# A fused attention and expert kernel: scores and their copies ranked ahead, three small steps moved to other engines

## The chip, the core and the metric

One core of one Trainium2 chip runs the whole program. Its engines work side by side, each on a queue of its own that it takes strictly in order: TensorE (PE: matrix products and transposes; PEld is its weight load), VectorE (DVE), ScalarE (ACT), GpSimd (POOL), and SyncE (SP), which here only issues transfers. The metric is the device time of one execution in microseconds (us).

## What is computed

```python
def reference(**kwargs):
    attn_out = _attn_ref(**attn_kwargs)          # 4 batches, 8 heads, 576 x 64
    x = np.ascontiguousarray(attn_out.transpose(0, 2, 1, 3)).reshape(B * S, H * D)
    x = _moe_ref(x=x, **moe_kwargs)              # (x @ w_a) * (x @ w_b) @ w_out, 512 -> 1536 -> 512
    return _moe2_ref(x=x, **moe2_kwargs)         # each token to one of 8 experts, 512 -> 1024 -> 512

def _attn_ref(q, k, v):
    top_k = 32
    scores = scale * np.matmul(q, k.transpose(0, 1, 3, 2))
    kth = np.partition(scores, -top_k, axis=-1)[..., -top_k:-top_k + 1]
    scores = np.where(scores >= kth, scores, -1000000000.0)
    scores = scores - np.max(scores, axis=-1, keepdims=True)
    attn = np.exp(scores)
    attn = attn / (np.sum(attn, axis=-1, keepdims=True) + 1e-09)
    return np.matmul(attn, v).astype(np.float32)
```

So every row of 576 scores keeps its 32 largest, and the first dense layer (w_a, w_b, w_out) follows, then the experts.

## The kernel before

**Tiles and loops.** A batch has four head pairs. A unit is one head pair of a batch, or, in batch 0, one head pair and one of two groups of rows (group 0 with 320 of the 576 rows, group 1 with 256). That gives 8 units in batch 0, of which the first four are group 0, and 4 units in each later batch. A unit's group has four tiles of 128 query rows (two for each head, taken in pairs) and group 0 a fifth one (kind "M"); there are 144 tiles, 36 per batch, in 32 groups.

**One pair of tiles** (`attn_tiles`, `attn_out`). TensorE makes scores of one half of the keys into the tile `sp` (one buffer in PSUM), ScalarE copies them to `s` (L527), TensorE makes the other half into the same `sp`, ScalarE copies that too. VectorE forms the larger and the smaller of the two halves (`m` and `n`, L534 and L535), finds the 32 largest by rounds of MAX8 and MATCH_REPLACE8 (L546 to L573), and makes the masked numerators `am` with their sums (L601). For the exponential (`e`, ScalarE, L554) GpSimd makes the negative scaled maximum `nm` (L549). TensorE transposes `am` (L609 to L636), ScalarE copies the transposes to `aT` (L616 to L638), and at a group's end TensorE multiplies them with v (`pv`, L648 and L652).

**Normalization** (`attn_norm`). GpSimd adds 1e-9 to the sums (L671), VectorE takes reciprocals (L673), ScalarE spreads them (L674, L682), TensorE turns them to rows in `pv` (L690, L692). In batches 0 and 1 ScalarE then copies these to `rs` (L697) and GpSimd multiplies `xf` out of `xc` and `rs` (L698); in batches 2 and 3 VectorE multiplies straight from PSUM (L701).

**The dense layer** (`moe1`). It starts for a batch (in batch 0 for a group) when `xf` is there: ScalarE and GpSimd split `xf` into a high part `xh` (L716) and a remainder `xl` (L718); TensorE multiplies with w_a and w_b (L748) and with w_out (L778), three products for each, as the weights are split too. Before that the weights, which arrive as 64-bit words, go through 36 conversions (`conv`, L371 to L424): a load, two ScalarE and two VectorE steps (L385, L388), a product on GpSimd (L391), the split (L396, L397) and stores to the scratch tensors `ws` and `wos`, from which `moe1` loads its weights into `wt` (three buffers). The conversions borrow the buffers gT, gH, xh and xl of `moe1`. After each batch or group `gating` sorts the rows into `xsort`; at the end the experts follow (L1109, L1158).

**What sets the order.** All of this is recorded as operations with an engine, an assumed cost and a rank `pos` (10 per tile). A planner (`Plan.emit`) walks through them by its assumed times: an engine that is free takes, of the operations that are ready, the one with the lowest rank. The instructions are then written out in the order of the planned starts. The dense layer's products have rank 100000 and more, so they fill what attention leaves free on TensorE; its evacuations have rank -1. On the chip each engine keeps that order, whether or not the first in its queue is ready.

Of the kernel before, what the change touches and what calls it, by code (L numbers as in the profile page):

```python
# [14 lines left out]
AF = mybir.ActivationFunctionType  # L15
OP = mybir.AluOpType
# [4 lines left out]
SCALE = 0.125  # L21
# [163 lines left out]
def c_act(n, sbuf=False):  # L185
    return (95 if sbuf else 55) + n * 0.83
# [23 lines left out]
def fused_kernel(ctx: ExitStack, tc: tile.TileContext, q, k, v, w_a, w_b, w_out, w_gate, w1, w2, qx, kx, vx, out,  # L210
                 opts=None, dbg=None):
    nc = tc.nc
    opts = opts or {}
# [15 lines left out]
    HB = FB // 2  # L229
    CW = 512  # L230
    HALVES = opts.get("halves", (0,))
    FU = opts.get("fu", range(8))
    PE, ACT, DVE, POOL, SP = "PE", "ACT", "DVE", "POOL", "SP"

# [17 lines left out]
    P = P_.op  # L252
# [115 lines left out]
    def conv(src, pos):  # L368
        (zr, raw), (zf, f) = conv_bufs()
        fk = ("f", nconv[0])  # L370
        o = P(SP, c_dma(128 * CW * 8), pos, lambda: nc.sync.dma_start(raw().bitcast(I64), src), w=[(zr, "r")])  # L371
        if nconv[0] > opts.get("c0", 2):
            o.deps.add(U[0].mark)

        def words(i):
            return raw().bitcast(I32).rearrange("p (n t) -> p n t", t=2)[:, :, i]

        def hi():
            return words(1).bitcast(F32)

        def fi():
            return f().bitcast(I32)
        P(ACT, c_act(CW, True), pos, lambda: nc.scalar.activation(f(), hi(), AF.Abs, scale=2.0 ** -111),
          r=[(zr, "r")], w=[(zf, fk)])
        P(DVE, c_ts(CW), pos, lambda: nc.vector.tensor_scalar(  # L385
            fi(), fi(), 3, 0x7fffffff, op0=OP.logical_shift_left, op1=OP.bitwise_and), w=[(zf, fk)])
        P(ACT, c_act(CW, True), pos, lambda: nc.scalar.activation(hi(), hi(), AF.Sign), w=[(zr, "r")])
        P(DVE, c_dve(CW), pos, lambda: nc.vector.scalar_tensor_tensor(  # L388
            fi(), words(0), 29, fi(), op0=OP.logical_shift_right, op1=OP.bitwise_or),
          r=[(zr, "r")], w=[(zf, fk)], label=f"cv{nconv[0]}")  # L390
        P(POOL, c_pool(CW), pos, lambda: nc.gpsimd.tensor_mul(f(), f(), hi()), r=[(zr, "r")], w=[(zf, fk)])  # L391
        return (zf, fk), f, zr, raw
# [93 lines left out]
    def attn_tiles(lst, r, pos):  # L486
# [8 lines left out]
        if kind == "M":  # L495
            sp = T(p_ps, [128, 2, 512], F32, "sp", 1)

            def score():
# [4 lines left out]
                                               kp()[:, 64 + hf * HS:64 + (hf + 1) * HS], start=(x == 0),  # L503
                                               stop=(x == len(pr) - 1))
                return res
            P(PE, 980 if u.f else 900, pos, score, r=u.q + u.k, w=[sp],
              label=f"score{u.b}")
            P(ACT, c_act(S), pos, lambda: nc.scalar.copy(
                s()[:, 0, :].rearrange("p (a b) -> p a b", a=2), sp()[:, :, 0:HS]), r=[sp], w=[(s, (0, 0)), (s, (0, 1))],
              label="s")  # L510
        else:
            for hf in range(2):
                sp = T(p_ps, [128, 2, 512], F32, "sp", 1)

                def score(hf=hf, sp=sp):
# [6 lines left out]
                                                   kp()[a, k0 + hf * HS:k0 + (hf + 1) * HS], start=(x == 0),  # L522
                                                   stop=(x == len(pr) - 1))
                    return res
                P(PE, 780 if u.f else 540, pos, score, r=u.q + u.k, w=[sp],
                  label=f"score{u.b}")
                P(ACT, c_act(S), pos, lambda hf=hf, sp=sp: nc.scalar.copy(  # L527
                    s()[:, :, hf * HS:(hf + 1) * HS], sp()[:, :, 0:HS]), r=[sp], w=[(s, (h, hf)) for h in range(2)],
                  label="s")

# [14 lines left out]
        for h, (i, j, kind, _, c) in enumerate(lst):  # L545
            P(DVE, c_dve(HS), pos, lambda h=h, j=j: nc.vector.max(out=kt(j, 0, 8), in_=m()[:, h]), r=[(m, h)],  # L546
              w=[KT(j, 0)])
        nm = T(p_sml, [128, 2, 1], F32, "nm", 3)
        P(POOL, 180, pos - 5, lambda: nc.gpsimd.tensor_scalar(  # L549
            nm()[:, 0:nh], r.kt()[:, j0:j0 + nh, 0:1], -SCALE, None, op0=OP.mult),  # L550
          r=[KT(j0 + h, 0) for h in range(nh)], w=[nm])
        for h, (i, j, kind, _, c) in enumerate(lst):
            e = T(p_at, [128, S], F32, "e", opts.get("e", 3))
# [106 lines left out]
        return any(a <= i < b and i % m < n for a, b, n, m in opts.get("mk", ()))  # L660

    def b_norm(b):
        return b in opts.get("pn", (0, 1))

    def attn_norm(i, r, xf, pos):
        u, g, nt = r.u, r.g, r.nt
# [1 line left out]
        P(POOL, 170, pos, lambda: nc.gpsimd.tensor_sub(  # L668
            chk_t[:, i - nt + 1:i + 1], r.kt()[:, 0:nt, 47], r.kt()[:, 0:nt, 39]),
          r=[r.kt], w=[(CHK, i)])  # L670
        P(POOL, 180, pos - 20, lambda: nc.gpsimd.tensor_scalar(r.sum()[:, 0:nt], r.sum()[:, 0:nt], 1e-9, None, op0=OP.add),  # L671
          w=[r.sum])
        P(DVE, 100, pos - 20, lambda: nc.vector.reciprocal(r.sum()[:, 0:nt], r.sum()[:, 0:nt]), w=[r.sum])  # L673
        P(ACT, c_act(256, True), pos - 20, lambda: nc.scalar.copy(  # L674
# [863 lines left out]
```

## Time and profile before

| | us |
|---|---|
| median of 3 runs (1207.56 to 1209.87) | 1208.23 |
| the profiled execution | 1207.8 |
| its span, first to last instruction | 1206.1 |
| TensorE busy | 1082.9 (90%) |
| VectorE busy | 894.5 (74%) |
| ScalarE busy | 678.6 (56%) |
| GpSimd busy | 462.5 (38%) |

The sum in the prediction is made against the profiled execution: 1207.8 us, of which 1.7 lie outside its span, and 0.4 below the median. Shares over the whole span mix stages with different limits: attention runs from 5 to 796 us, the dense layer from 142 to some 900, the experts after it. Times in rows count from the start of the span. "Granted clock" is the share of TensorE's full speed that was granted; its two levels are 1.2 and 2.4 GHz (0.5 and 1.0), so a mean of 0.85 tells that it stood at the lower level for 30% of the stretch.

### The profile page before, as it was taken

The page shows a single profiled execution, that of the slowest core. Times are in us where ns is not written, and L with a number is a line of the kernel's source. Part 1 is how long each engine was busy: PE and PEld are TensorE (multiplying, and loading weights), DVE is VectorE, ACT ScalarE, POOL GpSimd, SP SyncE. Part 2 cuts the span into 40 slices and gives each one's busy share as a digit, 9 for nine tenths or more (in the row PEclk, how much of TensorE's full clock was granted, in tenths as well). Part 3 has the DMA queues.
Part 4 walks back from the last instruction along what each step waited for, and adds up shares of the span by engine and source line. Part 5 has one row for each costly group of instructions (what it writes and reads, how often), then busy time and mean ns, then how long its engine had stood idle before and what let it go on. Part 6 is the DMA issues. An engine that isn't in the chain of part 4 may idle for free.

```text
span 1206.1 us, 21828 instructions
## 1 busy us (share of the span) xinstructions
PE 1082.9 (90%) x7586; PEld 942.3 (78%) x7586; DVE 894.5 (74%) x2636; ACT 678.6 (56%) x1442; POOL 462.5 (38%) x620
## 2 busy tenths in 40 slices
PE   3555696887999999999999999998999999999997
PEld 1333474765788789889888888898998999999996
DVE  6999999999989999999999999920005554544441
ACT  6667676775666666666666655723224454554551
POOL 3555577654445444134646313535134100000001
PEclk9766796987999999999999999999999999999999
DMA  7586577996666423333334242245735555554450
GB/s 260 172 311 200 177 250 252 364 311 205 233 235 208 171 96 114 135 115 120 130 104 137 79 144 78 80 167 206 253 126 177 180 151 191 179 163 148 160 177 21
DMA packets 90476, 210.47 MB, mean 175 GB/s; under 512 B 7363, under 2 KB 44611, under 8 KB 82677
## 3 DMA queue, kind: packets, MB, share of 16 engines
q1 hardware_dynamic: 87141, 199.53, 49.2%
q0 software_dynamic: 3216, 9.46, 2.1%
q8 instruction: 62, 1.02, 0.3%
q14 instruction: 57, 0.47, 0.1%
HBM read 174.31 MB, written 35.25 MB: 174 GB/s over the span
## 4 chain that ended last, share of the span: by engine, by line
PE 53%; DVE 23%; issue 9%; DMA 6%; ACT 4%; POOL 3%; SPq 0%; POOLq 0%; DVEq 0%; ACTq 0%
PE ab L748 18%; PE ab L778 10%; DVE m L559 5%; PE ab L1109 4%; DVE kt L562 4%; DVE am L601 4%; PE pv L648 3%; PE sp L521 3%; PE tp L627 3%; PE ms L1158 2%; PE pv L1158 2%; DMA xsort<-rows,pi 2%; DMA out_dram<-y,ti 2%; DVE m L535 1%; DVE n L535 1%
## 5 line engine op out<-in xcount | busy, mean ns | idle before, releaser
L748 PE MATMUL ab<-xh,wt 128*128 128x320 f32 (+1 forms) x1344 | 302.9, 306 | 3.9 <-ACT sb L733 3.9
L748 PEld LDWEIGHTS ab<-xh,wt 128*128 128x128 f32 x1344 | 226.3, 191 | 17.8 <-issue 11.1
L748 PE MATMUL ab<-xl,wt 128*128 128x320 f32 (+1 forms) x672 | 200.0, 298 | 1.4 <-POOL xl L718 1.4
L559 DVE MATCH_REPLACE8 m<-kt,m 128x288 f32<-128x288 f32 x432 | 188.5, 440 | 0.0
L562 DVE MAX8 kt<-m 128x8 f32<-128x288 f32 x432 | 182.1, 444 | 0.4
L778 PE MATMUL ab<-gH,wt 128*128 128x320 f32 (+1 forms) x768 | 169.4, 304 | 2.9 <-DMA wt<-wos 2.9
L756 POOL TENSOR_TENSOR sa<-sa,sb 128x320 f32<-128x320 f32 (+1 forms) x96 | 82.9, 864 | 154.9 <-ACT sb L733 147.8
L601 DVE SCALAR_TENSOR_TENSOR am<-s,kt,e 128x576 f32<-128x576 f32 x144 | 137.9, 983 | 0.0
L778 PEld LDWEIGHTS ab<-gH,wt 128*128 128x128 f32 x768 | 127.8, 190 | 10.7 <-issue 6.4
L748 PEld LDWEIGHTS ab<-xl,wt 128*128 128x128 f32 x672 | 128.9, 192 | 1.6 <-POOL xl L718 1.6
L554 ACT ACTIVATE e<-s,nm 128x576 f32<-128x576 f32 x144 | 108.9, 781 | 16.8 <-POOL nm L549 15.6
L778 PE MATMUL ab<-gT,wt 128*128 128x320 f32 (+1 forms) x384 | 113.8, 296 | 0.0
L1183 POOL DMA_INDIRECT out_dram<-y,ti x23 | 22.9, 997 | 227.6 <-ACT y L1177 208.7
L1027 DVE TENSOR_TENSOR wp<-raw,wp 128x1024 fp32r<-128x1024 f32 (+1 forms) x73 | 67.4, 943 | 52.8 <-ACT wp L1026 52.6
L527 ACT COPY s<-sp 128x576 f32<-128x576 f32 x128 | 81.9, 640 | 40.5 <-PE sp L521 37.5
L627 PE MATMUL tp<-idr,am 128*128 128x128 f32 x512 | 82.3, 299 | 19.4 <-DVE am L601 16.0
L397 POOL TENSOR_TENSOR gT<-sa,gH 128x320 fp32r<-128x320 f32 (+1 forms) x96 | 83.9, 874 | 40.6 <-ACT gH L396 40.4
L631 ACT COPY aT<-tp 128x512 f32<-128x512 f32 x128 | 71.4, 588 | 41.9 <-PE tp L627 41.6
L627 PEld LDWEIGHTS tp<-idr,am 128*128 128x128 f32 x512 | 63.0, 153 | 37.5 <-DVE am L601 18.9
L521 PE MATMUL sp<-rawk,rawq 64*128 64x288 f32 x128 | 37.6, 666 | 60.3 <-DVE n L534 21.9
L1109 PE MATMUL ab<-xgh,wp 128*128 128x304 f32 (+6 forms) x352 | 89.8, 313 | 1.5 <-DVE gT L1116 0.9
L648 PE MATMUL pv<-aT,vt 128*64 128x320 f32 (+1 forms) x512 | 80.4, 458 | 4.2 <-ACT aT L616 3.4
(280 smaller groups left out, 2409.0 us busy)
## 6 DMA issues: line engine op xcount, KB each, us to landing
wt<-ws SPq DMA_DIRECT2D x54, 1024.0 KB, 5.5
wt<-wos SPq DMA_DIRECT2D x44, 768.0 KB, 4.3
raw<-in_moe_w_dram SPq DMA_DIRECT2D x64, 512.0 KB, 3.8
xsort<-rows SPq DMA_DIRECT2D x8, 771.0 KB, 13.1
wp<-ws SPq DMA_DIRECT2D x6, 1024.0 KB
rawk<-in_kx_dram SPq DMA_DIRECT2D x19, 320.0 KB, 5.7
rawq<-in_qx_dram SPq DMA_DIRECT2D x19, 320.0 KB, 3.7
vt<-in_vx_dram SPq DMA_DIRECT2D x20, 288.0 KB, 2.8
```

Of the source, the lines that this page charges most:

```text
L397: P(POOL, c_pool(cost), pos, lambda: nc.gpsimd.tensor_sub(lo(), src(), fr(hi())), r=rd + wh, w=wl)
L527: P(ACT, c_act(S), pos, lambda hf=hf, sp=sp: nc.scalar.copy(s()[:, :, hf * HS:(hf + 1) * HS], sp()[:, :, 0:HS]), r=[sp], w=[(s, (h, hf)) f ...
L554: P(ACT, c_act(S, True) + 90, pos, lambda h=h, e=e: nc.scalar.activation(e(), s()[:, h], AF.Exp, bias=nm()[:, h], scale=SCALE), r=[(s, (h, ...
L559: P(DVE, c_dve(HS), pos + 5.0 * h, lambda x=x, h=h, j=j: nc.vector.match_replace(out=m()[:, h], in_to_replace=kt(j, 8 * x - 8, 8 * x), in_ ...
L562: P(DVE, c_dve(HS), pos + 5.0 * h, lambda x=x, h=h, j=j: nc.vector.max(out=kt(j, 8 * x, 8 * x + 8), in_=m()[:, h]), r=[(m, h)], w=[KT(j, x)])
L601: P(DVE, c_dve(S) + 60, pos, lambda: nc.vector.scalar_tensor_tensor(am(), sc(), kth(), e(), op0=OP.is_ge, op1=OP.mult, accum_out=r.sum()[: ...
L627: res = nc.tensor.transpose(tp()[:, 512 * h + x * 128:512 * h + (x + 1) * 128], z()[:, 640 * h + x * 128:640 * h + (x + 1) * 128], idf)
L648: nc.tensor.matmul(pv()[64 * h:64 * h + 64, 0:n], u.vt()[:, 256 * h + 64 * j:256 * h + 64 * j + 64], r.aT[h]()[:, j, 0:n], start=(j == 0), ...
L748: res = nc.tensor.matmul(pa()[:, 0:n], view()[:, m, wi, ko, :], xv()[:, ko], start=(ko == 0 and x == 0), stop=(ko == KO - 1 and x == 2))
L756: P(POOL, c_pool(n), pos, lambda: nc.gpsimd.tensor_mul(sa()[:, 0:n], sa()[:, 0:n], sb()[:, 0:n]), r=[sb], w=[sa])
L778: res = nc.tensor.matmul(pa()[:, 0:n], wv()[:, wi, f, :], gv()[:, f, :], start=(f == 0 and x == 0), stop=(f == HB - 1 and x == 2))
L1109: res = nc.tensor.matmul(pa()[:, 0:cap], p1[ko]()[:, wi, f * 128:(f + 1) * 128], xv()[:, ko], start=(ko == 0 and i == 0), stop=(ko == KO - ...
```

## The change

- Scores (TensorE) and their copies (ScalarE) get the rank of their pair less 30, three tiles ahead.
- The negative maximum `nm` is made by ScalarE in place of GpSimd (80 instructions).
- The addition of 1e-9 to the sums is made by VectorE in place of GpSimd (32 instructions).
- Batches 2 and 3 are normalized as batches 0 and 1 are: ScalarE copies `rs`, GpSimd multiplies (16 groups).
- Not in the title: all conversions' loads, the first two too, now come after the loads of the first unit's q and k.

```diff
+    SP_ = opts.get("spp", 30)
...
-        if nconv[0] > opts.get("c0", 2):
+        if nconv[0] > opts.get("c0", 0):
             o.deps.add(U[0].mark)
...
-            P(PE, 980 if u.f else 900, pos, score, r=u.q + u.k, w=[sp],
+            P(PE, 980 if u.f else 900, pos - SP_, score, r=u.q + u.k, w=[sp],
               label=f"score{u.b}")
-            P(ACT, c_act(S), pos, lambda: nc.scalar.copy(
+            P(ACT, c_act(S), pos - SP_, lambda: nc.scalar.copy(
...
-                P(PE, 780 if u.f else 540, pos, score, r=u.q + u.k, w=[sp],
+                P(PE, 780 if u.f else 540, pos - SP_, score, r=u.q + u.k, w=[sp],
                   label=f"score{u.b}")
-                P(ACT, c_act(S), pos, lambda hf=hf, sp=sp: nc.scalar.copy(
+                P(ACT, c_act(S), pos - SP_, lambda hf=hf, sp=sp: nc.scalar.copy(
...
-        P(POOL, 180, pos - 5, lambda: nc.gpsimd.tensor_scalar(
-            nm()[:, 0:nh], r.kt()[:, j0:j0 + nh, 0:1], -SCALE, None, op0=OP.mult),
+        P(ACT, 190, pos - 5, lambda: nc.scalar.activation(
+            nm()[:, 0:nh], r.kt()[:, j0:j0 + nh, 0:1], AF.Copy, scale=-SCALE),
...
-        return b in opts.get("pn", (0, 1))
+        return b in opts.get("pn", (0, 1, 2, 3))
...
-        P(POOL, 180, pos - 20, lambda: nc.gpsimd.tensor_scalar(r.sum()[:, 0:nt], r.sum()[:, 0:nt], 1e-9, None, op0=OP.add),
+        P(DVE, 70, pos - 20, lambda: nc.vector.tensor_scalar(r.sum()[:, 0:nt], r.sum()[:, 0:nt], 1e-9, None, op0=OP.add),
```

The planner makes a new order of all engines out of this. Line numbers in the changed kernel are one higher from L232 on.

ScalarE's first instructions after the table load, before (gT and gH are conversion buffers, L383 and L387 a conversion's two ScalarE steps):

```order
L383 ACTIVATE gT_135<-gT_135 128x512
L527 COPY s<-sp 128x2x288
L387 ACTIVATE gT_135<-gT_135 128x512
L383 ACTIVATE gH_137<-gH_137 128x512
L387 ACTIVATE gH_137<-gH_137 128x512
L527 COPY s<-sp 128x2x288
L396 CAST gT_135<-gT_135 128x512
```

And in the changed kernel:

```order
L528 COPY s<-sp 128x2x288 x2
L384 ACTIVATE gT_147<-gT_147 128x512
L550 ACTIVATE nm<-kt 128x2
L388 ACTIVATE gT_147<-gT_147 128x512
L555 ACTIVATE e<-s,nm 128x576
L528 COPY s<-sp 128x2x288
L555 ACTIVATE e<-s,nm 128x576
```

Both score copies of the first pair now stand ahead of the first conversion, and the negative maximum stands on ScalarE ahead of its exponentials.

TensorE in batch 1, second unit, from the first half of a pair's scores to the second half, before (kH, kL, qH, qL are k and q in two parts):

```order
L521 MATMUL sp<-kH,qL 128x288 x2
L521 MATMUL sp<-kL,qH 128x288 x2
L778 MATMUL ab<-gH_1335,wt 128x320
L778 MATMUL ab<-gT_1344,wt 128x320
L778 MATMUL ab<-gH_1335,wt 128x320 x2
L778 MATMUL ab<-gT_1344,wt 128x320
L778 MATMUL ab<-gH_1335,wt 128x320
L627 MATMUL tp<-idr,am 128x128 x8
L636 MATMUL pv<-idr,am 128x128
L521 MATMUL sp<-kH,qH 128x288 x2
L521 MATMUL sp<-kH,qL 128x288 x2
L521 MATMUL sp<-kL,qH 128x288 x2
```

And the same pair in the changed kernel:

```order
L522 MATMUL sp<-kH,qH 128x288 x2
L522 MATMUL sp<-kH,qL 128x288 x2
L522 MATMUL sp<-kL,qH 128x288 x2
L628 MATMUL tp<-idr,am 128x128 x8
L522 MATMUL sp<-kH,qH 128x288 x2
L522 MATMUL sp<-kH,qL 128x288 x2
L522 MATMUL sp<-kL,qH 128x288 x2
L637 MATMUL pv<-idr,am 128x128
```

Six products of the dense layer and one transpose no longer stand between the two halves.

SyncE at the end of the conversions, before (gT and gH hold the last two conversions, rawq and vt are loads for the third unit of batch 1, xsort fills scratch rows):

```order
L420 DMA wos<-gH_2335 128x4x128
L420 DMA wos<-gT_2322 128x4x128
L420 DMA wos<-gH_2335 128x4x128
L341 DMA xsort<-rows 96x4x514 x2
L766 DMA wt<-wos 128x1536 x3
L435 DMA rawq<-in_qx_dram 128x640
L435 DMA vt<-in_vx_dram 128x576
L766 DMA wt<-wos 128x1536
```

And in the changed kernel:

```order
L421 DMA wos<-gT_2268 128x4x128 x2
L342 DMA xsort<-rows 96x4x514
L436 DMA rawk<-in_kx_dram 128x640
L342 DMA xsort<-rows 96x4x514 x2
L436 DMA rawq<-in_qx_dram 128x640
L421 DMA wos<-gH_2373 128x4x128 x2
L436 DMA vt<-in_vx_dram 128x576
L767 DMA wt<-wos 128x1536 x4
```

The loads of rawq and vt now stand ahead of the dense layer's four loads from wos, rawq ahead of the last conversion's stores too.

## Rows read from the trace of the kernel before

**Rows 1.** Stretches of core 0: length, busy time (instructions) of PE PEld DVE ACT POOL; PEclk, DMA, GB/s

```profile
0.00:140.00 140.00, 75.38 (x296) 45.82 (x296) 129.19 (x383) 88.82 (x174) 68.81 (x98) 0.74 0.70 228
140.00:290.00 150.00, 117.31 (x732) 90.45 (x732) 148.90 (x433) 102.13 (x208) 96.23 (x100) 0.85 0.83 280
290.00:400.00 110.00, 107.64 (x865) 93.42 (x866) 102.34 (x335) 70.85 (x164) 49.32 (x77) 1.00 0.63 221
400.00:426.00 26.00, 21.91 (x154) 15.56 (x152) 26.00 (x94) 16.16 (x36) 12.97 (x18) 0.93 0.33 114
426.00:800.00 374.00, 371.81 (x2847) 323.23 (x2845) 345.34 (x1109) 230.53 (x521) 156.91 (x225) 1.00 0.33 114
800.00:1206.10 406.10, 388.81 (x2704) 373.82 (x2702) 142.70 (x288) 170.12 (x341) 78.21 (x104) 0.98 0.49 164
```

**Rows 2.** Waits of VectorE from 0 to 426 us: us in total, times, longest us

```profile
DVE m L535 <- ACT s L527: 7.9, 5, 3.8
DVE gT L385 <- ACT gT L383: 6.2, 1, 6.2
DVE sum L673 <- POOL sum L671: 1.6, 2, 1.0
DVE n L535 <- ACT s L527: 0.7, 1, 0.7
```

**Rows 3.** Timeline at 297 us: start, length, engine, instruction, [idle before <-releaser]

```profile
297.43 1.08 ACT L631 COPY aT<-tp 128x512 f32<-128x512 f32 x2 [1.31 <-PE tp L627]
...
298.55 0.67 ACT L527 COPY s<-sp 128x576 f32<-128x576 f32 x1
...
299.25 0.76 DVE L535 TENSOR_TENSOR m<-sp,s 128x576 f32<-128x576 f32 x1 [2.43 <-ACT s L527]
```

**Rows 4.** Timeline at the program's start

```profile
4.62 2.11 PE L521 MATMUL sp<-rawk,rawq 64*128 64x288 f32 x4 [4.62 <-DMA rawq<-in_qx_dram]
...
7.78 0.66 ACT L383 ACTIVATE gT<-gT 128x512 f32<-128x512 f32 x1 [5.68 <-DMA gT<-in_moe_w_a_dram]
8.34 0.63 ACT L527 COPY s<-sp 128x576 f32<-128x576 f32 x1
```

**Rows 5.** The moved steps and their likes, by line and form: busy us, mean ns

```profile
L673 DVE RECIPROCAL sum<-sum 128x5 f32<-128x5 f32 x16 | 2.9, 178 | 0.4 <-POOL sum L671 0.3
...
L619 ACT COPY aTt<-tp 64x64 f32<-64x64 f32 x16 | 3.3, 209 | 0.0
```

**Rows 6.** The same by line: ns shortest/median/longest, first and last start

```profile
L549 POOL TENSOR_SCALAR nm<-kt x80: 208/223/737, 14.7 to 781.6; 128x2 f32<-128x2 f32 x64, 128x1 f32<-128x1 f32 x16
...
L697 ACT COPY rs<-pv x16: 357/406/446, 51.8 to 423.7; 128x320 f32<-128x320 f32 x8, 128x256 f32<-128x256 f32 x8
...
L701 DVE TENSOR_TENSOR xf<-xc,pv x16: 417/442/487, 452.2 to 795.9; 128x320 f32<-128x320 f32 x8, 128x256 f32<-128x256 f32 x8
...
L698 POOL TENSOR_TENSOR xf<-xc,rs x16: 733/861/1245, 52.3 to 424.2; 128x320 f32<-128x320 f32 x8, 128x256 f32<-128x256 f32 x8
...
L601 DVE SCALAR_TENSOR_TENSOR am<-s,kt,e x144: 789/809/2052, 22.0 to 786.8; 128x576 f32<-128x576 f32 x144
```

**Rows 7.** Waits over the whole span: us in total, times, longest us

```profile
ACT e L554 <- POOL nm L549: 15.6, 21, 3.5
...
DVE xf L701 <- PE pv L690: 11.2, 6, 7.0
```

**Rows 8.** Timeline of SyncE and TensorE after the last conversion

```profile
274.54 4.33 SPq L766 DMA_DIRECT2D wt<-wos  x3
...
290.01 0.33 SPq L435 DMA_DIRECT2D vt<-in_vx_dram  x1
...
290.96 0.39 PE L778 MATMUL ab<-gH,wt 128*128 128x320 f32 x1
```

**Rows 9.** A piece of the chain that ended last (start, length) and a row of transfers (KB, us to landing)

```profile
870.08 21.12 PE ab L748 x144
...
wt<-wos SPq DMA_DIRECT2D x44, 768.0 KB, 4.3
```

## Prediction

> **What bounds the kernel now.** I read the busy times by stretch first. From 426 to 800 us TensorE is busy for 371.8 of 374 us and from 800 on for 388.8 of 406 [rows 1]; VectorE has 28.7 us of idle time in the first of these and is nearly unused in the second. There the end is set by how many products TensorE still has to do. Before 290 us it is the other way round: VectorE works for 148.9 of 150 us, while TensorE idles for 32.7 and stands at a granted clock of 0.85 [rows 1], because the dense layer cannot start before a batch's attention and its weights are ready. So the whole time is the moment from which TensorE is full for good, plus the work it then has left. That moment is about 426 us: the last product of batch 1's normalization starts at 424.2 (L698) [rows 6], and the dense layer of batch 1 needs it. In the 26 us before it TensorE has little of the dense layer left: busy 21.9, clock 0.93 [rows 1].
>
> So an edit gains where it brings batch 1's attention forward on VectorE, and only as far as TensorE has the rest of batch 0's dense layer done by then. What TensorE can get back between 290 and 426 is 110 - 107.6 = 2.4 us, 26 - 21.9 = 4.1 us, and 26 x (1 - 0.93) = 1.8 us of clock, together **8.3 us** [rows 1]. Second I read VectorE's waits up to 426 us [rows 2], third the timeline at one of them [rows 3] and at the start [rows 4], last the rows of the steps that change engine.
>
> **Scores and copies ahead.** VectorE waits 7.9 + 0.7 = 8.6 us for the copy s before 426 us [rows 2]. The timeline shows how: two copies of transposes run on ScalarE from 297.43 for 1.08 us, a shorter one follows, the score copy starts only at 298.55, and VectorE's m starts at 299.25 after 2.43 us of nothing [rows 3]. On TensorE six products of the dense layer and nine transposes stood between the two halves of those scores; in the new order eight transposes are left, and on ScalarE the shorter copy falls behind the score copy. The gain lies between 0 (TensorE itself is late, and the copy waits for it) and 8.6; I take 6.0, about what the waits over 2 us make up, since the order attacks those. The same rank moves work on TensorE: before the attention product that ends the second unit of batch 1, 366 of the products at L748 stood in its queue, now 330. That is 36 products behind attention, at 21.12 / 144 = 0.147 us each [rows 9] **5.3 us**, out of a stretch where TensorE is full into the one where it is short of work.
>
> **The start.** The first copy could run when the first scores end, 4.62 + 2.11 = 6.73, but it stands behind a conversion that waits 5.68 us for its load and starts at 8.34 [rows 4]. Now both copies are first, up to 1.6 us earlier. VectorE, which used part of that time for conversions, must do these later, so I count 0.6, between 0 and 1.6. The loads of the first two conversions are issued behind five more transfers; their results are needed only at 142 us, so this is worth nothing, and would cost ScalarE a wait at the most, with no VectorE work behind it.
>
> **The sums.** VectorE no longer waits 1.6 us for GpSimd's addition [rows 2], but makes 16 additions before 426 us. At the length of a reciprocal of the same shape, 0.178 us [rows 5], they cost 2.8 us if nothing overlaps. Bounds -1.6 and +2.8; I take 0, between them, since a short step mostly starts while the one ahead of it is still ending.
>
> **The negative maximum.** 80 steps of 0.223 us leave GpSimd [rows 6]; on ScalarE the nearest row is a 64x64 copy of 0.209 us [rows 5], so 80 x 0.209 = 16.7 us over 780 us. ScalarE is busy for 278 of the first 426 us and 230.5 of the next 374 [rows 1]; that idle time hides it. The exponential waited 15.6 us for the step on GpSimd [rows 7]; now both are neighbours in one queue. If nm must wait for VectorE's maximum there, evacuations of TensorE's results wait behind it, but behind the exponential they stood in the same way. Zero, between -1 and +2 us (a tenth of the 15.6 each way, rounded).
>
> **Normalization in batches 2 and 3.** It takes 16 x 0.442 = 7.1 us off VectorE and the waits of 11.2 us for the turned reciprocals [rows 6, 7], adds 16 x 0.406 = 6.5 us to ScalarE and 16 x 0.861 = 13.8 us to GpSimd (busy 157 of 374) [rows 1, 6]. All of it is after 426 us, where TensorE sets the pace: zero. Without that cover the last group's chain would be 0.406 + 0.861 - 0.442 = 0.8 us longer.
>
> **SyncE.** The load of vt now stands ahead of all four loads of w_out's second half. Before, it was issued at 290.01, when its buffer came free, while the first three of those loads had gone at 274.54; the products that use them started at 290.96 [rows 8]. Behind vt the first load can go at 290.34 and lands 4.3 us later [rows 9], at 294.6, which is 3.7 us late. If attention is 4 us earlier by then, the buffer is too, and it costs nothing; if not, 8.3 - 3.7 = 4.6 us are left for TensorE to regain. I keep 0 to 3.7.
>
> **Sum.** VectorE reaches the end of batch 1 some 6.0 + 0.6 = 6.6 us earlier, TensorE has 5.3 us of work put where it was short and at least 4.6 us of room for it. The smaller side counts: -5 us against the profiled 1207.8, so 1202.8; that execution lies 0.4 below the median of the runs, which gives **1203.2**, said as 1203. The best case is the whole 8.3 plus 1.6 of the start, 1198.
>
> **Rivals.** *A, the copies are not VectorE's real wait* (no change). TensorE is busy for 107.6 of 110 us from 290 to 400 [rows 1], so the scores may come late because TensorE is, and ranking them only trades places. Then only the six products between the halves count, 0.9 us at the two long waits: 1206.4 to 1207, within the bound of 0.2% (2.4 us), which is about what a measurement of this kernel can tell from no change. Against it: VectorE's waits name the copy, and one of its causes, the copies of transposes, is on ScalarE [rows 3].
>
> *B, TensorE stalls at its head* (slower). A score may start only when VectorE has read the one score buffer. Ranked ahead, it reaches the head of TensorE's queue the sooner, and if VectorE is later than the planner assumed, the dense layer's products behind it wait too. Batches 2 and 3 have 72 such score blocks, in a stretch where TensorE now idles for 2.2 us in all [rows 1]. At 0.15 us each this is 10.8 us: 1207.8 - 5 + 10.8 + 0.4 = 1214. It decides from (5 + 2.4) / 72 = 0.10 us a block. For it speaks that TensorE does idle between 140 and 290; against it that scores already ranked above the dense layer.
>
> *C, GpSimd's products hold off VectorE* (no change). The masking step L601 takes 0.809 us in the median and up to 2.052 [rows 6], and the added products could fall beside it: 16 x 1.24 = 19.8 us at the worst, less the 7.1 saved, 12.7 later at the end of batch 3. VectorE waited 7.0 us there [rows 7], so 5.7 would show and eat the gain: 1208. It needs nearly every product to hit. The Trainium skill, SBUF — State Buffer, section Who interferes with whom, speaks for this one: an instruction of VectorE with two SBUF inputs and one of GpSimd that reads SBUF exclude each other, while one with a single SBUF input, as the replaced multiplication out of PSUM is, does not. By that rule the move trades a harmless step for one that locks; the trace's spread at L601 fits it, but no row here shows a lock by itself.
>
> **How the numbers follow.** Forecast 0.58, with a larger gain (1198 to 1200) another 0.03; A 0.21; C 0.05; B 0.13. Faster by over 0.2% is 0.61, within it 0.26, slower 0.13. The range takes in the best case, A and C with a little more: 1198 to 1210; B stays outside.
>
> **What would show it.** Right: VectorE's waits for s before 426 us fall from 8.6 us to about 3; batch 1's last normalization starts near 418 instead of 424.2; TensorE is busier between 400 and 420; from 426 on its idle time stays near 2 us. The start is right if m no longer follows two conversions. Wrong: the last normalization of batch 1 moves, but TensorE's idle time only shifts (SyncE's loads or rival A); TensorE idles before scores after 426 us (B); L601's mean grows after 426 us (C).

## The result and the profile after

| | before | after |
|---|---|---|
| median, us (4 runs each, side by side) | 1208.84 (1207.56 to 1209.87) | 1215.22 (1214.26 to 1215.97) |
| ratio to before, 95% interval | | **1.0053** (1.0035 to 1.0070) |
| the profiled execution / its span, us | 1207.8 / 1206.1 | 1214.3 / 1212.5 |

The changed kernel is slower by 0.5%. The forecast was 1203 with a range of 1198 to 1210, so the time lies outside it and on the other side. The first view is the one the prediction began with, the stretches; these rows answer to [rows 1] (busy us with instruction counts of PE, PEld, DVE, ACT, POOL, then PEclk, DMA share, GB/s).

```profile
0.00:140.00 140.00, 75.31 (x292) 44.97 (x292) 127.48 (x383) 90.38 (x187) 66.35 (x81) 0.71 0.71 225
140.00:290.00 150.00, 119.57 (x738) 91.86 (x736) 148.19 (x422) 101.68 (x220) 94.61 (x81) 0.87 0.81 270
290.00:400.00 110.00, 106.87 (x812) 91.48 (x811) 104.52 (x347) 71.31 (x170) 42.15 (x55) 0.94 0.61 216
400.00:426.00 26.00, 24.15 (x191) 18.59 (x190) 25.40 (x95) 17.69 (x43) 12.31 (x14) 1.00 0.48 180
426.00:800.00 374.00, 368.71 (x2812) 318.35 (x2813) 351.14 (x1121) 242.62 (x577) 156.05 (x188) 1.00 0.32 111
```

Read the product counts of TensorE against [rows 1]. Up to 290 us nothing is lost (292 for 296, 738 for 732). From 290 to 400 TensorE starts 812 products where it started 865: **53 are missing**, with an idle time of 3.1 us for 2.4 and a clock of 0.94 for 1.00. From 400 to 426 it catches up 37 of them (191 for 154). From 426 to 800 it loses 35 again (2812 for 2847), with 5.3 us idle for 2.2. The balance at 426 us is -4 + 6 - 53 + 37 = -14 products, at 800 us -49; at the 0.147 us of [rows 9] the latter is 7.2 us, an estimate (the kinds are mixed), against the 6.4 us by which the span is longer. The stretch from 400 to 426 us, where TensorE was short of work before, takes back most of what was missing; 20 of the 35 lost afterwards go by 430 us, while TensorE stands and batch 1's dense layer is not there yet (last row of the timeline below).

The waits of VectorE up to 426 us, which answer to [rows 2]:

```profile
DVE m L536 <- ACT s L528: 11.3, 5, 7.3
DVE n L536 <- ACT s L528: 3.1, 4, 0.9
DVE m L536 <- PE sp L522: 2.2, 1, 2.2
```

The waits for scores did not go away. 7.3 of the 11.3 us is the program's start, which before was booked under a conversion (6.2 us, [rows 2]). Without the start there are 4.0 + 3.1 + 2.2 = 9.3 us, where there were 8.6 (one more wait of m, 1.0 us, is named after a copy of transposes).

The timeline of the kernel after at five places: the first score step, an addition on VectorE, ScalarE ahead of the last conversion, SyncE and TensorE at the start of the dense layer's second half, and the last normalization of batch 1 with TensorE's wait beside it.

```profile
9.62 0.76 DVE L536 TENSOR_TENSOR m<-sp,s 128x576 f32<-128x576 f32 x1 [7.31 <-ACT s L528]
...
202.97 1.36 POOL L398 TENSOR_TENSOR gH<-gH 128x512 fp32r<-128x512 f32 x1 [0.73 <-ACT gH L397]
203.13 1.23 DVE L672 TENSOR_SCALAR sum<-sum 128x4 f32<-128x4 f32 x1
...
270.63 0.20 ACT L550 ACTIVATE nm<-kt 128x2 f32<-128x2 f32 x1 [3.00 <-DVE kt L547]
...
271.18 0.68 ACT L384 ACTIVATE gH<-gH 128x512 f32<-128x512 f32 x1
...
279.70 0.37 SPq L421 DMA_DIRECT2D wos<-gH  x1
287.27 0.35 SPq L436 DMA_DIRECT2D vt<-in_vx_dram  x1
287.73 1.33 SPq L767 DMA_DIRECT2D wt<-wos  x3
292.77 0.61 PE L779 MATMUL ab<-gH,wt 128*128 128x320 f32 x1
...
427.69 0.74 POOL L699 TENSOR_TENSOR xf<-xc,rs 128x256 f32<-128x256 f32 x1
...
428.64 0.53 PE L503 MATMUL sp<-kH,qH 128*128 128x288 f32 x2 [2.10 <-DVE n L536]
```

Batch 1's last normalization starts at 427.69 instead of 424.2 [rows 6], 3.5 us later, where 418 was forecast. The loads from wos go at 287.73 instead of 274.54 [rows 8], and the last store that they need only at 279.70: the last conversion begins on ScalarE at 271.18, behind a negative maximum that waits 3.00 us for VectorE. TensorE stands for 2.10 us up to 428.64. The addition at 203.13 lasts 1.23 us; it ends when GpSimd's step ends.

### The profile page after: what moved, and what is told of

Same layout as the page of the kernel before. It is cut to its first block, busy times and chain, and to the rows that moved or that the text cites. A ratio compares the mean times of both kernels' runs of the same rounds, so it can differ in the third digit from the quotient of the medians.

```text
span 1212.5 us, 21783 instructions
## 1 busy us (share of the span) xinstructions
PE 1089.3 (90%) x7586; PEld 944.1 (78%) x7586; DVE 899.3 (74%) x2652; ACT 694.5 (57%) x1538; POOL 451.6 (37%) x524
## 4 chain that ended last, share of the span: by engine, by line
PE 53%; DVE 26%; issue 8%; DMA 6%; ACT 5%; POOL 2%; SPq 1%; POOLq 0%; DVEq 0%; ACTq 0%
PE ab L749 18%; PE ab L779 9%; DVE m L560 6%; DVE am L602 5%; DVE kt L563 5%; PE ab L1110 5%; PE tp L628 3%; PE sp L522 3%; PE ms L1159 3%; PE pv L1159 3%; PE pv L649 3%; DMA xsort<-rows,pi 2%; DVE n L536 2%; DVE m L536 2%; DVE kt L547 1%
## 5 line engine op out<-in xcount | busy, mean ns | idle before, releaser
L749 PEld LDWEIGHTS ab<-xh,wt 128*128 128x128 f32 x1344 | 227.0, 192 | 18.3 <-issue 11.3
L779 PE MATMUL ab<-gH,wt 128*128 128x320 f32 (+1 forms) x768 | 173.8, 308 | 2.7 <-DMA wt<-wos 2.7
L602 DVE SCALAR_TENSOR_TENSOR am<-s,kt,e 128x576 f32<-128x576 f32 x144 | 146.9, 1045 | 0.0
L779 PEld LDWEIGHTS ab<-gH,wt 128*128 128x128 f32 x768 | 130.6, 194 | 11.3 <-issue 7.6
L628 PE MATMUL tp<-idr,am 128*128 128x128 f32 x512 | 86.3, 303 | 15.8 <-DVE am L602 9.9
```

The source lines that it names most:

```text
L602: P(DVE, c_dve(S) + 60, pos, lambda: nc.vector.scalar_tensor_tensor(am(), sc(), kth(), e(), op0=OP.is_ge, op1=OP.mult, accum_out=r.sum()[: ...
L628: res = nc.tensor.transpose(tp()[:, 512 * h + x * 128:512 * h + (x + 1) * 128], z()[:, 640 * h + x * 128:640 * h + (x + 1) * 128], idf)
L749: res = nc.tensor.matmul(pa()[:, 0:n], view()[:, m, wi, ko, :], xv()[:, ko], start=(ko == 0 and x == 0), stop=(ko == KO - 1 and x == 2))
L779: res = nc.tensor.matmul(pa()[:, 0:n], wv()[:, wi, f, :], gv()[:, f, :], start=(f == 0 and x == 0), stop=(f == HB - 1 and x == 2))
```

## The experiments

Theories at the outset: the *lock* (VectorE's additions wait for GpSimd), the *scores* (ranking them ahead holds up other work), the *products* (GpSimd's new ones lengthen L601), and the *order* (the planner places thousands of rows anew, and what is lost is lost by that). Ratios are to the kernel before, run beside each kernel on the same chip; its median there was 1206.0 to 1207.0 us.

### Each part alone

```diff
s_scores: +    SP_ = opts.get("spp", 30)      (scores and copies at pos - SP_)
s_add:    -        P(POOL, 180, ... nc.gpsimd.tensor_scalar(r.sum()...
          +        P(DVE, 70, ... nc.vector.tensor_scalar(r.sum()...
s_nm:     -        P(POOL, 180, ... nc.gpsimd.tensor_scalar(nm()...
          +        P(ACT, 190, ... nc.scalar.activation(nm()...
s_norm:   -        return b in opts.get("pn", (0, 1))
          +        return b in opts.get("pn", (0, 1, 2, 3))
```

> Scores and their copies ranked ahead by 30, nothing else changed. Lock theory (the slowdown is VectorE's addition, which takes 0.145 us alone but 0.32 to 1.23 us beside a GpSimd step): this part alone is not slower, 1204 to 1209. Score theory (ranking the scores ahead holds back other work): 1212 to 1216, most of the 6.4 us. Order theory (any new order of the planner moves the conversions' end and the half-clock stretch, whatever the part): anything from 1204 to 1215, read from where the half-clock stretch near 290 us lies.

> Only the addition of 1e-9 is made by VectorE. Lock theory: 16 additions before 426 us take about 6.5 us of VectorE there, so batch 1's last normalization ends 3 to 6 us later than 424.9 and the time is 1211 to 1214. Score theory: within 2 us of before, 1206 to 1210. Order theory: no relation to the additions' own duration.

> Only the negative maximum is made by ScalarE. Lock and score theories: GpSimd loses 80 short steps, VectorE nothing; 1205 to 1210. Order theory: could leave this by as much as the others.

> Only batches 2 and 3 are normalized by GpSimd. Nothing before 426 us is touched but through the planner's order. If the part is worth nothing, as predicted: 1206 to 1210. If GpSimd's added products hold off L601: its mean after 426 us grows from 0.97 by 0.1 us or more, and the time is 1210 to 1213. Order theory: batch 1's end moves although no step before it has changed.

| kernel | median, us | ratio (95%) |
|---|---|---|
| s_scores | 1209.69 | 1.0024 (1.0012 to 1.0036) |
| s_add | 1217.56 | 1.0080 (1.0052 to 1.0109) |
| s_nm | 1214.53 | 1.0060 (1.0040 to 1.0080) |
| s_norm | 1212.79 | 1.0054 (1.0033 to 1.0074) |

Every part alone is slower, and the four losses together (2.2%) are four times that of all of them at once. Costs that belong to the steps would add up; these don't. Two steps that should hardly matter, the negative maximum and the normalization behind TensorE's cover, cost 0.6% and 0.5%. That speaks for the order, which each of them changes as a whole. The *products* theory does not carry s_norm: the masking steps L601 after 426 us are busy for 70.82 us (72 steps) against 66.93 (71 steps) before, 0.04 us a step more where 0.1 was its sign.

In s_scores the waits that the change was to remove are nearly all there (first two rows: VectorE, up to 426 us; m was 7.9 and n 0.7), and the last normalization of batch 1 starts at 422.9 us, 1.3 earlier than before (third row), without a gain in the time:

```profile
DVE m L536 <- ACT s L528: 6.7, 5, 2.7
...
DVE n L536 <- ACT s L528: 0.7, 1, 0.7
```

```profile
L699 POOL TENSOR_TENSOR xf<-xc,rs x1: 734/734/734, 422.9 to 422.9; 128x256 f32<-128x256 f32 x1
```

### The order kept and the engine moved, and the reverse

The planner still counts the step as the old engine's, so all other queues keep their rows, and only the instruction goes to the new engine (f_). Or the planner counts it as the new engine's, and the instruction stays on the old one (g_).

```diff
f_add: -   P(POOL, 180, pos - 20, lambda: nc.gpsimd.tensor_scalar(r.sum()...
       +   P(POOL, 180, pos - 20, lambda: nc.vector.tensor_scalar(r.sum()...
g_add: +   P(DVE, 70, pos - 20, lambda: nc.gpsimd.tensor_scalar(r.sum()...
f_nm:  +   P(POOL, 180, pos - 5, lambda: nc.scalar.activation(nm()...
f_all: f_add and f_nm, and in batches 2 and 3
       +   P(DVE, c_dve(n), pos - 20, lambda: (nc.scalar.copy(rs()...), nc.gpsimd.tensor_mul(xf()...))[1],
```

> The addition runs on VectorE, but the planner still counts it as GpSimd's: every other queue keeps the order of the kernel before. Lock theory: the 10.6 us of s_add are the addition's own, so this loses 6 to 10 us too (1213 to 1217). Order theory: what s_add lost came from the new order; left are the 16 additions before 426 us, 2.3 us if none waits for GpSimd and 6.5 at the length they had in the changed kernel, less the 1.6 us of waiting that goes: 1207.5 to 1212, in the middle 1209.

> The reverse: the order of s_add word for word on the other queues, but the addition runs on GpSimd as in the kernel before. Lock theory: the loss of s_add is gone, 1206 to 1209. Order theory: most of it stays, 1212 to 1217, and VectorE idles for about 11 us between 300 and 430 us as in s_add (5.2 before).

> The negative maximum runs on ScalarE, the planner still counts it as GpSimd's; VectorE, TensorE and SyncE keep the order of before. Order theory: 1205 to 1209, the step itself costs nothing. If the step itself costs what s_nm lost (ScalarE's copies of scores wait behind a step that waits for VectorE's maximum): 1212 to 1215, and VectorE's idle time between 300 and 430 us grows from 5.2 to about 12 us.

> All three steps on their new engines (addition, negative maximum, normalization of batches 2 and 3), the planner's order that of the kernel before, scores not ranked ahead. Order theory: 1206 to 1212, below the changed kernel by 3 us or more. If the moves themselves carry the slowdown: 1214 or more.

| kernel | order | engines | median, us | ratio (95%) |
|---|---|---|---|---|
| f_add | before | addition moved | 1209.13 | 1.0019 (1.0005 to 1.0033) |
| g_add | that of s_add | as before | 1216.88 | 1.0083 (1.0066 to 1.0100) |
| f_nm | before | nm moved | 1207.01 | 1.0002 (0.9992 to 1.0013) |
| f_all | before | all three moved | 1210.70 | 1.0032 (1.0021 to 1.0043) |

g_add has no step on a new engine and loses as much as s_add: **in s_add the order alone is the 0.8%**. In the old order the addition costs 0.19%, 2.3 us, and the negative maximum nothing. f_all leaves about 0.0032 - 0.0019 - 0.0002 = 0.1% for the normalization, by difference and not by a run of its own.

### The whole change, its order with the old engines

```diff
g_addnm (from the changed kernel):
-   P(DVE, 70, pos - 20, lambda: nc.vector.tensor_scalar(r.sum()...
+   P(DVE, 70, pos - 20, lambda: nc.gpsimd.tensor_scalar(r.sum()...
-   P(ACT, 190, pos - 5, lambda: nc.scalar.activation(nm()...
+   P(ACT, 190, pos - 5, lambda: nc.gpsimd.tensor_scalar(nm()...
```

> The order of the changed kernel on every queue, but the additions and the negative maximum run on GpSimd again. Order theory: with the additions' own 2.3 us (f_add) and nothing for the negative maximum (f_nm) the time is 1211 to 1214, still 4 us or more above the kernel before. If the slowdown is the additions' waits for GpSimd: 1206 to 1209.

> The changed kernel again, for comparison with g_addnm on the same chip: 1213 to 1216.

g_addnm took 1215.66 us, 1.0071 (1.0052 to 1.0090); the changed kernel beside it 1214.19, 1.0060 (1.0043 to 1.0077). Two of the three moved steps are undone and nothing comes back, not even the 2.3 us that was expected: in this order VectorE waits for GpSimd's addition instead. The stretch from 290 to 400 us is as poor as in the changed kernel. First its row of that stretch, then that wait (up to 426 us):

```profile
290.00:400.00 110.00, 104.84 (x814) 89.66 (x815) 103.37 (x340) 69.32 (x156) 45.92 (x72) 0.97 0.60 210
```

```profile
DVE sum L674 <- POOL sum L672: 3.9, 4, 1.9
```

The stretch in f_all, the moved steps in the old order, has the products of before (862 for 865):

```profile
290.00:400.00 110.00, 107.32 (x862) 93.03 (x862) 103.17 (x342) 73.12 (x179) 44.61 (x60) 1.00 0.63 225
```

What f_all loses, 4 us, it loses elsewhere. Its last normalization of batch 1 starts at 422.4 us, 1.8 earlier than before, but after 426 us it starts 2806 products up to 800 us for 2847. The largest piece lies from 640 to 660 us (first row; before in the second), where TensorE idles for 3.05 us, waiting for a copy on ScalarE (1.7 us) and for VectorE's masking (1.2). Which of the moved steps brings that about stays open.

```profile
640.00:660.00 20.00, 16.95 (x134) 14.21 (x134) 19.64 (x58) 12.52 (x29) 11.56 (x15) 1.00 0.26 87
```

```profile
640.00:660.00 20.00, 19.92 (x158) 17.54 (x159) 19.40 (x64) 12.66 (x29) 10.45 (x16) 1.00 0.33 102
```

### Which part of the order

Candidates were the late loads on SyncE and the half-clock stretch that follows in the changed kernel. Its two stretches, the second of them at half the clock throughout:

```profile
284.00:290.50 6.50, 4.32 (x32) 2.56 (x31) 6.50 (x21) 3.80 (x9) 3.28 (x4) 1.00 0.34 108
290.50:304.20 13.70, 11.68 (x51) 9.94 (x50) 13.53 (x46) 6.76 (x15) 0.20 (x1) 0.50 0.35 143
```

TensorE was busy for 4.32 of 6.5 us and then stood at 1.2 GHz for 13.7 us, in which it started 51 products. In the kernel before, the half-clock stretch came while it was still short of dense work. Three kernels try these causes:

```diff
x_bvt (from before; SyncE's queue alone): 
+        for d in range(3):
+            wo = at[f"wo0(0,){d}1"]          # the first three loads from wos
+            order.remove(wo)
+            order.insert(order.index(at["vt12"]) + 1 + d, wo)
x_vt (from the changed kernel; SyncE's queue alone):
+        order.remove(vt)
+        order.insert(order.index(at["wo0(0,)31"]), vt)
x_fill (from the changed kernel): 28 times, at six places of TensorE's queue
+        nc.tensor.matmul(pa()[:, 0:128], idr, idr, start=True, stop=True)
```

> The kernel before with SyncE's queue alone changed: the first three loads from wos now behind the load of vt, as in the changed kernel. They go at about 290.4 instead of 274.5 us and land at 294.7, so the second half starts 3.7 us later (294.7 for 291.0). By the load alone: 1210 to 1211. Clock theory: TensorE's poor stretch is longer by as much, and if the clock falls once more in it, 3 to 7 us are lost besides: 1213 to 1217.

> The changed kernel with one transfer moved: the load of vt issued behind three of the four loads from wos instead of ahead of them; all other queues as they are. The loads then go at about 284, when the last store has landed, and land at 288.5 instead of 292.4. Clock theory: TensorE has dense work again 2 us before its clock would fall; if the clock holds, 6 us or more come back (1207 to 1210), and if it falls a little later all the same, 1 to 3 us (1212 to 1214). Rival, the load's place by itself: 4 us and no change of the clock, 1211.

> The changed kernel with 28 products of 128 columns put into TensorE's queue between the end of the dense layer's first half (284.0 us) and the first product of its second half (292.8 us); their results are overwritten. Clock theory (the loss is the half-clock stretch from 290.5 to 304.2 us, which follows 6.5 us with TensorE busy for 4.3): the clock is held, or its fall comes elsewhere, the second half of batch 0's first group ends 5 to 7 us earlier than in the changed kernel, and the time is 1207 to 1210. Rival, the attention's later end (428.4 us against 424.9) sets the time: within 1 us of the changed kernel, 1213 to 1216, even if the clock is held.

| kernel | median, us | ratio (95%) |
|---|---|---|
| x_bvt | 1213.40 | 1.0066 (1.0049 to 1.0082) |
| x_vt | 1213.91 | 1.0067 (1.0048 to 1.0087) |
| x_fill | 1215.74 | 1.0081 (1.0063 to 1.0098) |

x_bvt, in which nothing but three loads has another place in a queue, loses as much as the whole change. First SyncE and TensorE in its timeline:

```profile
289.89 0.36 SPq L440 DMA_DIRECT2D vt<-in_vx_dram  x1
290.42 1.28 SPq L771 DMA_DIRECT2D wt<-wos  x3
294.69 0.41 PE L783 MATMUL ab<-gH,wt 128*128 128x320 f32 x1 [3.60 <-DMA wt<-wos]
```

Then the stretch from 290 to 400 us, 45 products short of before, and VectorE's wait for scores up to 426 us:

```profile
290.00:400.00 110.00, 103.98 (x820) 90.08 (x819) 97.69 (x319) 67.20 (x155) 46.90 (x73) 0.98 0.65 228
```

```profile
DVE m L540 <- ACT s L532: 12.9, 6, 7.1
```

The second half starts 3.7 us later, as [rows 8] let one work out. The scores that stand between its products in TensorE's queue are late with it, and after the wait TensorE stood at half its clock for a while (first row; before, these 4 us had a clock of 1.00). VectorE waits 12.9 us for scores instead of 7.9, and the wait that ended at 299.25 [rows 3] now ends at 304.53 (second row):

```profile
294.00:298.00 4.00, 3.31 (x14) 3.27 (x14) 3.40 (x11) 0.00 (x0) 0.60 (x1) 0.62 0.95 389
```

```profile
304.53 0.76 DVE L540 TENSOR_TENSOR m<-sp,s 128x576 f32<-128x576 f32 x1 [7.06 <-ACT s L532]
```

VectorE is 5.3 us late there: 3.7 from the loads and, by estimate, 4 x (1 - 0.62) = 1.5 from the clock. Batch 1's last normalization starts at 429.5, also 5.3 us later than before. So the transfer's lateness is passed on to VectorE, with some lost clock on top, as the clock theory had it for this kernel; where the other 2 us of the 7.4 arise is not shown.

x_fill gains nothing, although its clock is at 0.88 in the stretch in which the changed kernel stood at half speed. That stretch, and TensorE in it:

```profile
290.50:304.20 13.70, 9.18 (x58) 7.42 (x57) 13.53 (x44) 6.50 (x13) 1.07 (x2) 0.88 0.29 104
```

```profile
296.08 0.40 PE L533 MATMUL sp<-kH,qH 64*128 64x288 f32 x2 [3.30 <-DVE kt L585]
```

The second execution of the changed kernel, r_after, shows the same without any filling:

```profile
290.50:304.20 13.70, 9.29 (x56) 7.36 (x55) 13.53 (x44) 6.07 (x13) 1.07 (x2) 0.88 0.36 135
```

```profile
296.85 0.40 PE L522 MATMUL sp<-kH,qH 64*128 64x288 f32 x2 [3.29 <-DVE kt L574]
```

That it is the filling that raised the clock is therefore not shown. But the clock theory falls for this stretch all the more: r_after's execution took 1212.33 us with a clock of 0.88 there, the first one 1214.26 with 0.50, and runs of r_after alone lie as far apart. With the higher clock TensorE does a group of 12 dense products (by 292.8 us in x_fill) and then stands for 3.3 us at a score that waits for VectorE, with the next dense products behind it; what it does faster it waits longer. x_vt brings the loads forward by only 2 us (285.60 for 287.73), since they must wait for the last store as well, and gains nothing either. The next two kernels take both causes of the late loads away.

```diff
y_after (from the changed kernel): x_vt's edit, and for the last conversion's steps and stores
+        for o in self.ops[CV36[0]:CV36[1]]:
+            o.start -= 8000
y_nm (from s_nm): x_vt's edit
```

> The changed kernel with the steps and stores of the last conversion put 8 us earlier in the order of their queues and the load of vt behind the first three loads from wos; nothing else is moved. The loads from wos go at 274 to 279 instead of 287.7 us, the second half of the dense layer starts at about 284.5 instead of 292.8. Weights theory (the late loads from wos carry the slowdown): batch 0's first group is done 6 to 10 us earlier than at 325.1 and the time is 1206 to 1210. Rival, the rest of the new order (scores at the head of TensorE's queue, the additions, ScalarE's waits) carries it: 1212 to 1216.

> The kernel with only the negative maximum on ScalarE (s_nm, 1214.5 us, whose stores to wos end at 274.4 us) with the load of vt behind the first three loads from wos. The loads go at 277 to 281 instead of 285.8 us. Weights theory: most of its 7.6 us come back, 1206 to 1210. Rival, the rest of its order: 1212 to 1216.

y_after took 1215.35 us, 1.0075 (1.0047 to 1.0102), and y_nm 1212.83, 1.0055 (1.0037 to 1.0074): the rival holds in both. y_after shows why. The loads go at 280.04 and TensorE still starts the second half at 290.54, because its queue has those products behind attention steps, and again it stands at a score:

```profile
280.04 2.97 SPq L778 DMA_DIRECT2D wt<-wos  x3
290.02 0.66 PE L639 MATMUL tp<-idr,am 128*128 128x128 f32 x4 [0.68 <-ACT aT L643]
...
290.54 0.39 PE L790 MATMUL ab<-gH,wt 128*128 128x320 f32 x1
...
296.05 0.40 PE L533 MATMUL sp<-kH,qH 64*128 64x288 f32 x2 [3.50 <-DVE kt L585]
```

In the changed kernel's program 36 dense products fewer stand in TensorE's queue ahead of the attention product that ends batch 1's second unit (330 of L748 for 366, as the prediction counted). Attention runs at VectorE's pace there; what does not stand between its steps cannot be done, whenever the weights land. That the places of the dense products carry the rest of the loss is what these runs point to; no kernel puts those products back alone, so this last link is argued.

### The stall behind the scatter

The study of TensorE's idle time turned up one that both kernels have. In the kernel before, these rows of the timeline, and the stretch that follows:

```profile
839.34 0.59 ACT L955 COPY rows<-ms 128x512 f32<-128x512 f32 x1 [4.62 <-DMA xsort<-rows,pi]
839.82 0.44 ACT L733 ACTIVATE sb<-ab 128x320 f32<-128x320 f32 x1
...
840.31 0.58 PE L748 MATMUL ab<-xh,wt 128*128 128x256 f32 x1 [3.46 <-ACT sb L733]
```

```profile
839.10:845.90 6.80, 5.59 (x23) 5.59 (x24) 0.00 (x0) 2.45 (x6) 4.49 (x7) 0.50 0.35 103
```

The one buffer of rows is still being scattered; the copy into it waits on ScalarE, the evacuation of TensorE's result waits behind the copy, TensorE waits for the evacuation, and its clock is at half for the next 6.8 us. A second buffer, with the planner's order as it was:

```diff
-        z = Lazy(lambda: pool().tile(shape, dt, name=name, bufs=bufs), bufs)
+        n = 2 if name == "rows" else bufs
+        z = Lazy(lambda: pool().tile(shape, dt, name=name, bufs=n), bufs)
```

> The kernel before, the planner's order kept, with a second buffer for the rows that are scattered after the dense layer. At 836.85 us TensorE idles for 3.46 us (behind an evacuation on ScalarE that stands behind a copy waiting 4.62 us for a scatter), and its clock is at half for the 6.8 us that follow. Clock theory: both go, 3.5 + 3.4 = 6.9 us, so 1200 to 1203. If only the wait goes: 1203 to 1205. If the next transfer is late anyway: no change.

> The changed kernel with the second buffer for scattered rows, its order kept. It idles at the same place for 2.8 us and its clock is at half for 3.4 us there, so 2.8 + 1.7 = 4.5 us or more come back (1209 to 1211), as against 8 us in the kernel before. If the gain there came from elsewhere: no change.

x_rows took **1197.41 us, 0.9934** (0.9917 to 0.9950): faster than both kernels, and by more than was expected. a_rows, the same in the changed kernel, took 1209.24, 1.0017 (1.0007 to 1.0027), 5 us below the 1214.19 of the changed kernel beside it. In x_rows the wait is gone and the clock stays up there. The stretch around the stall before (first row) and in x_rows (second row):

```profile
836.00:850.00 14.00, 10.54 (x62) 10.34 (x61) 0.00 (x0) 3.79 (x10) 5.52 (x8) 0.76 0.41 148
```

```profile
836.00:850.00 14.00, 14.00 (x105) 14.00 (x105) 0.00 (x0) 4.00 (x10) 5.55 (x7) 1.00 0.50 168
```

That is 43 products more, 6.3 us at 0.147 us each. The expectation's 3.5 + 3.4 us counts a little twice, since the stretch at half clock begins at 839.1, before the wait ends at 840.31: the wait of 3.46 us and half of the 5.59 us that TensorE is busy at half clock make the same 6.3 us.

## Why the prediction was wrong, by its own steps

**The frame held in one direction only.** Kernels whose last normalization of batch 1 starts 5 us or more later than 424.2 lose 0.55% to 0.83% (x_bvt 429.5, y_nm 430.1, g_add 431.3, s_add 433.6, s_nm 433.8); in the changed kernel it is 3.5 us later. But an earlier one gained nothing: s_scores (422.9) and f_all (422.4) are slower, f_nm (422.6) is as before. So bringing batch 1's attention forward by 1 to 2 us was worth nothing by itself. Even "TensorE busier from 400 to 420" came true (24.15 for 21.91 us from 400 to 426, clock 1.00 for 0.93); it was catching up, not getting ahead.

**Scores ahead: the step that failed.** It was counted at 6.0, with nothing below 0 in its bounds, on the reading that a wait named after the copy s ends when the copy is ranked higher. Alone it is 0.24% slower (about 2.9 us), and m's wait fell by 1.2 us only. Rival A fits this: TensorE, busy for 107.6 of 110 us there [rows 1], is itself late. At the very wait that the prediction read, TensorE still ran the scores until 298.10 (the row below, before), and the copy that stood behind the transposes' copies started at 298.55 [rows 3]: of the 2.43 us only some 0.45 lay on ScalarE.

```profile
297.81 0.29 PE L521 MATMUL sp<-kL,qH 64*128 64x288 f32 x2
```

The bound of 0 left out that a rank rewrites every queue. The 36 products "behind attention" did move to where they were wanted (37 more from 400 to 426 us), but were booked as pure help: the places that they left between attention's steps from 290 us on were not filled, and TensorE stood there or ran at half its clock.

**SyncE: the right place, the price too small.** Worked out were 294.6 us for the first product and 0 to 3.7 us of loss. x_bvt gave 294.69 and 7.4 us (0.66%, interval 0.49% to 0.82%). The term stopped at TensorE and left out the scores behind it and the clock after the wait. In the changed kernel the loads were late a second time through the last conversion's stores.

**The start.** m starts at 9.62, with no conversion ahead of it, where it started behind two; the first normalization starts no earlier for it, as the next row says beside [rows 6] (52.3), for the conversions' steps must be done all the same. 0.6 was counted, 0 is left.

```profile
L699 POOL TENSOR_TENSOR xf<-xc,rs x32: 729/870/1402, 52.6 to 796.9; 128x320 f32<-128x320 f32 x16, 128x256 f32<-128x256 f32 x16
```

**The sums.** Taken were 0 and a length of 0.178 us, with 2.8 as the upper bound. In the old order they cost 2.3 us (interval 0.6 to 4.0), near that bound. Their row in the kernel after, ns shortest, median and longest:

```profile
L672 DVE TENSOR_SCALAR sum<-sum x32: 142/156/1230, 42.1 to 788.6; 128x5 f32<-128x5 f32 x16, 128x4 f32<-128x4 f32 x16
```

The median is shorter than the reciprocal, but the mean is not: by form 7.1 + 4.8 us for 32, or 0.37 us each.

```profile
L672 DVE TENSOR_SCALAR sum<-sum 128x4 f32<-128x4 f32 x16 | 7.1, 446 | 0.0
...
L672 DVE TENSOR_SCALAR sum<-sum 128x5 f32<-128x5 f32 x16 | 4.8, 297 | 0.0
```

The Trainium skill, SBUF — State Buffer, section Who interferes with whom, names `tensor_scalar` among the operations of VectorE that can take the ports it shares with GpSimd; whoever comes first holds them for its whole instruction. The trace agrees: 1.23 us beside a GpSimd step, both ending within 0.03 us (204.36 and 204.33), and 0.14 to 0.16 us where no GpSimd step ran. Of the 32 additions 14 began during a GpSimd step and ended within 0.04 us of its end; one, at 633.60, took 0.14 us beside one. The prediction used this section for rival C and passed over the sentence on the operation that the change itself adds.

**The negative maximum** was right: zero forecast, 1.0002 measured, 206 ns a step for the 209 taken. That holds for the order of before; in the changed order one of its waits, 3.00 us at 270.63, delays the last conversion.

```profile
L550 ACT ACTIVATE nm<-kt x80: 190/206/254, 13.1 to 782.5; 128x2 f32<-128x2 f32 x64, 128x1 f32<-128x1 f32 x16
```

**Normalization** costs about 0.1% by difference, for a forecast of zero. Rival C's sign is there in part: VectorE's masking steps between 426 and 800 us are busy for 73.77 us in the first row below (after), for 66.93 before (second row), about 6 us more for one step more (a step is two of the counted instructions). VectorE idles for 22.9 us there, but that this covers it is not shown: f_all, with the same move, loses its products in that stretch.

```profile
426.00:800.00 374.00, 73.77 (x144) 1.00 0.32 111
```

```profile
426.00:800.00 374.00, 66.93 (x142) 1.00 0.33 114
```

**Rivals.** B gave 1214 and named the mechanism, TensorE standing at a score with dense products behind it. It was placed after 426 us, at 72 small waits; r_after, x_fill and y_after show it at 296 us, in single waits of 3.3 to 3.5 us, where VectorE sets the pace. After 426 us TensorE's idle time grew as well, from 2.2 to 5.3 us, but most of that is the one wait at 428.64, when batch 1's dense layer had no `xf` yet either. Its chance of 0.13 was too low mainly because the forecast took attention to be nearer and no term stood for a worse order.

## What to carry to other kernels

When a planner sets the order, price the new order before the edit: compare how many products stand between the steps of the slow engine, and which transfers now queue behind one that waits for a buffer. Separate the two by experiment: keep the order and move the engine, then the reverse; here the first cost 0.3%, and the second, with two of the three moved steps back on their old engines, left the whole loss in place. A wait of the engine that sets the end, with its clock low afterwards, is worth more than any of the small steps; look for a single buffer behind it.

## What the runs showed of the hardware beyond that

- VectorE's addition on 128x4 or 128x5 elements takes 0.14 to 0.16 us alone and up to 1.23 us when a GpSimd step is running; the reciprocal on the same tile, its neighbour in the queue, stays between 0.15 and 0.18.
- The same kernel had another clock in the same stretch in two executions: 0.50 from 290.5 to 304.2 us in one, 0.88 in the other (r_after). A clock seen in one profile, of a kernel with filling products for instance (0.88 too), needs a second one beside it before a cause is given.
- Removing a wait of 3.46 us gave back 8 us of 1206 (interval 6 to 10): 6.3 us of that, by estimate, are the wait and the half clock around it. The rest was gained earlier; of it, 1.7 us is another wait of TensorE's for a copy into the same buffer, between 290 and 426 us.
